# Retention and feed-forward on one core: first products of two blocks by turns, and all weights converted before the second products

## Chip, core and metric

The kernel runs on one core of a Trainium2 chip. The time is the device time of one execution, in microseconds (us); lower is better. The engines named below are PE (TensorE: matmuls), DVE (VectorE), ACT (ScalarE), POOL (GpSimd) and SP (SyncE, which here only issues DMAs).

## What is computed

A retention layer (attention without softmax, with a decay per head) over 8 batches, 8 heads, 576 positions and head size 64, and behind it a feed-forward layer with g = h - tanh(h). All in float32.

```python
def _attn_ref(q, k, v):
    scores = scale * np.matmul(q, k.transpose(0, 1, 3, 2))
    Dmat = np.where(rel >= 0, gamma[:, None, None] ** rel[None, :, :], 0.0)
    return np.matmul(scores * Dmat[None, :, :, :], v)

def _moe_ref(x, w_in, w_out):          # x: 4608 x 512
    h = x @ w_in                       # w_in: 512 x 2048
    g = h - np.tanh(h)
    return g @ w_out                   # w_out: 2048 x 512
```

## The kernel before

**Tiles.** The 576 positions are cut into 9 blocks of 64. One block of all 8 batches is 512 rows of x (`BLK`), kept transposed in two parts, `xh` and `xl`, a rounded value and the rest, since matmuls run on float32r. The 2048 columns of the hidden layer are 16 slices `f` of 128. For block n and slice f there are two groups of twelve 128x512 matmuls: the first product `mm1(n, f)` (line 249: 4 with `xh`, 4 with `xl`, 4 with `xh` and the weight's low part) writes h into a PSUM bank, tag "h", two buffers; the second product `mm2(n, f)` (line 298) adds to four output banks, tags "o0" to "o3". Eight PSUM banks are all there are: two "h", four "o", "new" and "own".

**Attention.** It runs by pairs of batches. `entry(p)` does the 64x64 matmuls of pair p: the outputs and the state of pair p, and the scores of pair p + 1. Then it copies (`after_score`, `after_out`, the state), issues the 1 MB load of pair p + 2 (`load_pair`, line 145; two buffers, so the load waits until pair p's matmuls are done) and has POOL scale q and v of that pair in place (`prep`, lines 154 and 155). Pairs 0 to 3 (block 0) are done by batch ahead of everything (`first_score`, the loop over j). Pairs 4 to 7 give block 1, pairs 8 to 11 block 2.

**Weights.** They arrive as 64-bit numbers and are turned into a high and a low float32r part on the chip, one 128x512 slice at a time: `guard` (two ACT instructions, lines 74 and 75, into a mask), `unit` (DVE, lines 83, 88 and 90, then an ACT cast, line 93), and `finish` (DVE, line 100, the low part), which comes behind the next weight's line 83. A call of `step()` issues a third of that. `stream` is the order: 16 slices of w_in, then 16 of w_out, slices 14 and 15 first (`turn`). `upto("load", n)` issues the loads of raw weights on SP.

**Before the weights are there.** While weights are converted, the first products of blocks 0 and 1 run, and ACT copies each h to SBUF and SP stores it in HBM (`spill`, lines 254 and 255). For (1, 14) and (1, 15) alone `activate` computes g at once. Then come 31 second products: block 1 in the order of `turn`, then block 0 (`late`). `fetch` reads a spilled h back four groups ahead and `resume` computes g, in its parts `gh` and `gl`, one group ahead. From block 2 on first and second products alternate and nothing is spilled.

**What sets the order.** The program is written in the order in which each engine runs it: `in_order` ties each instruction to the one before it on its engine. So an engine that waits holds back all that stands behind it, SP's issues too.

**Names in the change.** `lead`, `seq`: the list of first products by steps k. `bank`: the PSUM tag of h. `scores_of`: the PSUM bank of an entry's scores. `last_two`: the two steps in front of the second products. `ob`, `obs`: the SBUF copy of the output banks; tag "cv", three buffers, is shared with the masks and with `th` of `resume`; tag "xl", two buffers, holds the `xl` of two blocks.

Of the kernel before, what the change touches and what calls it, by code (L numbers as in the profile page):

```python
# [19 lines left out]
P = 128  # L20
# [29 lines left out]
def retention_ffn(ctx: ExitStack, tc: tile.TileContext, ins, out, spill):  # L50
# [57 lines left out]
    def upto(what, n):  # L108
        while at_[what] < min(n, 2 * NF):
            {"load": load_w, "guard": guard}[what](*stream[at_[what]])  # L110
            at_[what] += 1

    def step():

        if not going:
            if at_["convert"] == 2 * NF:
                return finish()
            upto("guard", at_["convert"] + 1)
            going.append(unit(at_["convert"]))
            at_["convert"] += 1  # L120
        if next(going[0], "end") == "end":
            going.pop()

    def units(n):
        while at_["convert"] < min(n, 2 * NF) or going:
            step()
# [32 lines left out]
    def half(k):  # L159
        return slice(64 * k, 64 * k + 64)  # L160
# [79 lines left out]

    gs, ops = {}, {}

    def mm1(n, f):
        hp = psp.tile([P, BLK], F32, tag="h", bufs=2, name=f"h{n}_{f}")
        xh, xl = xs[n]
        k = 0
        for a, x in ((0, xh), (0, xl), (1, xh)):
            for cc in range(NCC):
                nc.tensor.matmul(hp, win[f][:, a, cc, :], x[:, cc, :], start=(k == 0), stop=(k == 3 * NCC - 1))  # L249
                k += 1  # L250
        g = pool.tile([P, BLK], F32, tag="g", bufs=3, name=f"g{n}_{f}")
        if n == 0 or n == 1 and f < NF - 2:

            nc.scalar.copy(g, hp)
            nc.sync.dma_start(spill[n, f], g)
        else:
            activate(n, f, hp, g)
# [27 lines left out]
    def mm2(n, f):  # L285
        gh, gl = gs.pop((n, f))
        first, final = (turn[0], turn[-1]) if n == 1 else (0, NF - 1)
        if f == first:
            ops[n] = [psp.tile([P, DM], F32, tag=f"o{t}", bufs=1, name=f"o{n}_{t}") for t in range(4)]
        o = ops[n]  # L290
        terms = [(gh, 0), (gh, 1), (gl, 0)]
        if f != final:
            order = [(t, k) for k in range(3) for t in range(4)]
        else:
            order = [(t, k) for t in range(4) for k in range(3)]
        for t, k in order:
            g, a = terms[k]
            nc.tensor.matmul(  # L298
                o[t], g[:, t * P : (t + 1) * P], wout[f][:, a, :],
                start=(f == first and k == 0), stop=(f == final and k == 2),  # L300
            )
            if f == final and k == 2:
                ob = pool.tile([P, DM], F32, tag="cv", bufs=3, name=f"ob{n}_{t}")
                if t % 2 == 0:
                    nc.scalar.copy(ob, o[t])
                else:
                    nc.vector.tensor_copy(ob, o[t])
                for u in range(2):
                    nc.sync.dma_start(out[2 * t + u, n * C : (n + 1) * C], ob[half(u)])


    warm = const.tile([P, BLK], BF16, tag="wi15", name="warm")
# [42 lines left out]
    for j in range(B):  # L355
        if j < B - 1:
            first_score(j + 1)
        new = psp.tile([P, 8, D], F32, tag="h", bufs=2, name=f"new_first{j}")[:, :4]
        o = psp.tile([P, 8, C], F32, tag=f"o{2 + j % 2}", bufs=1, name=f"own_first{j}")[:, :4]
        run(m_state(j, new), m_out(j, o))  # L360
        if j < B - 2:
            busy(1, 64)
        if j == B - 1:
            busy(4)
        if 3 <= j < 6:
            step()
        after_out(j, o.unsqueeze(1), 1)
        nc.scalar.copy(state[:, j], new)
    units(2)
    prep(B // 2)  # L370
    prep(B // 2 + 1)

    def scores_of(n, f):

        return psp.tile([P, 2, 4, C], F32, tag=f"o{f % 4}", bufs=1, name=f"s{n}_{f}")

    p = B // 2
    late = [(1, f) for f in turn] + [(0, f) for f in range(NF)]
    for n in range(2):
        for f in range(NF):  # L380
            upto("load", 10 + 3 * f // 4 if n == 0 else NF + 5 + f)
            if n == 0 or f % 4 < 3:
                step()
            if n == 1 and f >= NF - 2:
                fetch(*late[f - NF + 4])
            mm1(n, f)
            if n == 0 or f % 4 < 3:
                step()
                step()
            if n == 0 and f == 2:  # L390
                sc = scores_of(n, f)
                run(m_score(B, sc[:, 0]) + m_score(B + 1, sc[:, 1]), [])
                after_score(B, sc, 2)
            if f in ((5, 8, 11, 14), (1, 5, 9, 13))[n]:
                entry(p, scores_of(n, f))
                p += 1
    for k, (n, f) in enumerate(late):
        for _ in range(2):
            step()
        if 0 < k < len(late) - 1:  # L400
            resume(*late[k + 1])
        if k + 4 < len(late):
            fetch(*late[k + 4])
        if k < len(late) - 1:
            mm2(n, f)

# [63 lines left out]
```

## Time and profile before

| what | value |
|---|---|
| time, median of 3 runs | 911.64 us (911.03 to 911.86) |
| the profiled execution | 914.6 us |
| its span, first to last instruction | 912.8 us |
| PE busy | 882.5 us (97%) |
| DVE / ACT / POOL busy | 369.9 (41%) / 281.1 (31%) / 90.4 (10%) us |
| DMA | 82.06 MB, mean 90 GB/s |
| mean granted clock of PE | 0.992 of full speed |

PE busy, granted clock and DMA rate by stretch:

| stretch, us | PE busy, us | DVE busy, us | granted clock | GB/s |
|---|---|---|---|---|
| 20 to 30 | 6.37 of 10 | 5.24 | 0.83 | 405 |
| 30 to 40 | 7.76 of 10 | 9.65 | 1.00 | 202 |
| 50 to 60 | 9.79 of 10 | 9.58 | 1.00 | 310 |
| 60 to 70 | 9.09 of 10 | 9.24 | 1.00 | 260 |
| 70 to 80 | 8.77 of 10 | 9.20 | 1.00 | 260 |
| 90 to 100 | 10.00 of 10 | 9.15 | 1.00 | 218 |
| 100 to 110 | 7.87 of 10 | 9.84 | 0.86 | 290 |
| 110 to 120 | 10.00 of 10 | 7.82 | 0.97 | 319 |
| 140 to 150 | 7.10 of 10 | 7.32 | 1.00 | 154 |
| 150 to 160 | 7.31 of 10 | 7.76 | 0.83 | 55 |
| 240 to 800 | 560 of 560 | | 1.00 | |

A busy share says little of the whole, since the stages differ: the attention of block 0 ends at about 24 us, first products of blocks 0 and 1 run from 25.46 to 144.22, the 31 second products to 239.76 (from 201.55 on without a gap), and from there first and second products alternate. The chain of waits, followed back from the last instruction, is 86% PE, 7% DVE, 2% ACT and 2% DMA.

### The profile page before, as it was taken

To read this page: it belongs to the slowest core of one execution; us is meant where nothing else is said; L and a number is where in the kernel's file an instruction comes from. 1 tells how busy PE (TensorE), PEld (TensorE's weight loads), DVE (VectorE), ACT (ScalarE), POOL (GpSimd) and SP (SyncE) were. 2 spreads that over 40 slices of the span, in tenths; PEclk is the share of its full clock that TensorE was granted. 3 is DMA by queue.
4 is the path that set the end of the run, shared out by engine and by line. 5 is a ranking of instruction groups with operands and counts; after the bars stand their busy time and mean duration, and the time that the engine had idled before them with its cause. 6 is when DMAs were issued, how large, how long until landed. Compare 5 with 4: busy or idle time off the path is not lost.

```text
span 912.8 us, 17584 instructions
## 1 busy us (share of the span) xinstructions
PE 882.5 (97%) x7832; PEld 722.0 (79%) x7832; DVE 369.9 (41%) x543; ACT 281.1 (31%) x482; POOL 90.4 (10%) x84
## 2 busy tenths in 40 slices
PE   6899997999999999999999999999999999999997
PEld 4677785778888888888888888888888888888885
DVE  3899877545322333223322333223332322223222
ACT  3665554444322222222222222222222222222222
POOL 4212221000011111111111111000111111000000
PEclk9999999999999999999999999999999999999999
DMA  9777783243211113111311131113000211002001
GB/s 355 272 264 246 251 314 105 98 122 105 63 54 52 48 47 93 53 48 47 93 53 47 47 93 53 47 48 93 32 32 38 80 60 47 1 1 47 1 1 46
DMA packets 30524, 82.06 MB, mean 90 GB/s; under 512 B 3696, under 2 KB 4848, under 8 KB 30448
## 3 DMA queue, kind: packets, MB, share of 16 engines
q1 hardware_dynamic: 30448, 80.94, 26.8%
q8 instruction: 61, 1.00, 0.4%
q14 instruction: 15, 0.12, 0.0%
HBM read 63.62 MB, written 17.30 MB: 89 GB/s over the span
## 4 chain that ended last, share of the span: by engine, by line
PE 86%; DVE 7%; ACT 2%; DMA 2%; issue 1%; SPq 1%; POOL 0%; ACTq 0%; DVEq 0%
PE o L298 42%; PE h L249 38%; PE s L191 3%; PE new L191 2%; PE own L191 2%; DMA a<-in_qkv_dram 1%; DVE wi L100 1%; DVE mi L88 1%; DVE mo L90 1%; DMA out_dram<-ob 1%; DVE mo L88 1%; DVE mi L90 1%; DVE wo L100 0%; DVE mi L83 0%; ACT wi L93 0%
## 5 line engine op out<-in xcount | busy, mean ns | idle before, releaser
L249 PE MATMUL h<-xh,wi 128*128 128x512 f32 x1152 | 308.5, 392 | 7.7 <-ACT wi L93 3.8
L298 PE MATMUL o<-wo,gh 128*128 128x512 f32 x1152 | 293.8, 393 | 8.7 <-ACT gh L281 3.7
L249 PEld LDWEIGHTS h<-xh,wi 128*128 128x128 f32 x1152 | 215.3, 188 | 56.3 <-ACT wi L93 5.7
L298 PEld LDWEIGHTS o<-wo,gh 128*128 128x128 f32 x1152 | 214.1, 188 | 56.7 <-ACT gh L281 5.2
L263 DVE TENSOR_TENSOR g<-h,g 128x512 f32<-128x512 f32 x114 | 78.8, 691 | 369.8 <-ACT g L262 369.8
L262 ACT ACTIVATE g<-h 128x512 f32<-128x512 f32 x114 | 68.2, 598 | 424.0 <-PE h L249 424.0
L298 PE MATMUL o<-wo,gl 128*128 128x512 f32 x576 | 159.2, 391 | 0.0
L249 PE MATMUL h<-xl,wi 128*128 128x512 f32 x576 | 154.6, 390 | 0.0
L298 PEld LDWEIGHTS o<-wo,gl 128*128 128x128 f32 x576 | 108.7, 189 | 22.7
L249 PEld LDWEIGHTS h<-xl,wi 128*128 128x128 f32 x576 | 108.3, 188 | 22.8
L265 DVE TENSOR_TENSOR gl<-g,gh 128x512 fp32r<-128x512 f32 x114 | 80.0, 702 | 78.2 <-ACT gh L264 71.4
L154 POOL TENSOR_TENSOR a<-a,qtab 128x512 f32<-128x512 f32 x32 | 42.9, 1339 | 663.2 <-DMA a<-in_qkv_dram 618.4
L264 ACT CAST gh<-g 128x512 fp32r<-128x512 f32 x114 | 70.7, 620 | 87.2 <-DVE g L263 87.2
L191 PE MATMUL own<-a,state 64*64 64x64 f32 x1024 | 63.1, 221 | 0.0
L191 PE MATMUL own<-pm,a 64*64 64x64 f32 x1024 | 61.4, 218 | 0.0
L191 PEld LDWEIGHTS own<-a,state 64*64 64x64 f32 x1024 | 51.2, 135 | 0.4 <-issue 0.4
L191 PEld LDWEIGHTS own<-pm,a 64*64 64x64 f32 x1024 | 51.3, 135 | 0.0
L191 PEld LDWEIGHTS s<-a 64*64 64x64 f32 x1024 | 32.6, 135 | 11.9 <-issue 10.5
L155 POOL TENSOR_TENSOR a<-a,vtab 128x512 f32<-128x512 f32 x32 | 37.8, 1182 | 0.0
L191 PE MATMUL s<-a 64*64 64x64 f32 x1024 | 37.0, 222 | 0.2 <-POOL a L154 0.2
L282 DVE TENSOR_TENSOR gl<-s,gh 128x512 fp32r<-128x512 f32 x30 | 20.8, 692 | 35.5 <-PE o L298 28.1
L191 PE MATMUL new<-a 64*64 64x64 f32 x896 | 30.8, 218 | 0.0
(46 smaller groups left out, 447.4 us busy)
## 6 DMA issues: line engine op xcount, KB each, us to landing
a<-in_qkv_dram SPq DMA_DIRECT2D x32, 1024.0 KB, 5.0
out_dram<-ob SPq DMA_DIRECT2D x72, 128.0 KB, 2.4
rwi<-in_w_in_dram SPq DMA_DIRECT2D x16, 512.0 KB, 9.2
rwo<-in_w_out_dram SPq DMA_DIRECT2D x16, 512.0 KB, 5.5
spill_dram<-g SPq DMA_DIRECT2D x30, 256.0 KB, 3.2
s<-spill_dram SPq DMA_DIRECT2D x30, 256.0 KB, 2.5
a<-in_qkv_dram SPq DMA_DIRECT2D x8, 512.0 KB, 7.6
qtab<-in_qtab_dram SPq DMA_DIRECT2D x9, 128.0 KB, 2.1
```

The lines of the kernel that those rows point to most:

```text
L88: nc.vector.scalar_tensor_tensor(z, lw, 29, z, op0=ALU.logical_shift_right, op1=ALU.bitwise_or)
L90: nc.vector.scalar_tensor_tensor(z, hw, -0x40000000, z, op0=ALU.bitwise_and, op1=ALU.bitwise_or)
L154: nc.gpsimd.tensor_tensor(a[:, :, 0], a[:, :, 0], qtabs[c].unsqueeze(1).broadcast_to([P, 2, 4, C]), op=ALU.mult)
L155: nc.gpsimd.tensor_tensor(a[:, :, 2], a[:, :, 2], vtab[:, c].unsqueeze(1).unsqueeze(3).broadcast_to([P, 2, 4, D]), op=ALU.mult)
L191: nc.tensor.matmul(out_, w, x, start=start, stop=stop)
L249: nc.tensor.matmul(hp, win[f][:, a, cc, :], x[:, cc, :], start=(k == 0), stop=(k == 3 * NCC - 1))
L262: nc.scalar.activation(g, h, AF.Tanh)
L263: nc.vector.tensor_tensor(g, h, g, op=ALU.subtract)
L264: nc.scalar.copy(gh, g)
L265: nc.vector.tensor_tensor(gl, g, gh.bitcast(F32), op=ALU.subtract)
L282: nc.vector.tensor_tensor(gl, g, gh.bitcast(F32), op=ALU.subtract)
L298: nc.tensor.matmul(o[t], g[:, t * P : (t + 1) * P], wout[f][:, a, :], start=(f == first and k == 0), stop=(f == final and k == 2),)
```

## The change

- First products are listed in `seq`: block 0 alone for ten steps, then blocks 0 and 1 by turns, then the last ten of block 1. Each of the 30 steps before the last two issues three calls of `step()`, so all 32 weights are converted (but for the last low part) when the second products begin.
- h goes to four banks in turn up to the fifth last step: the two of "h", and "o2" and "o3", which no second product uses yet. Scores of entries then use only "o0" and "o1".
- Pairs 4 to 7 have their entries behind steps 2, 4, 6 and 9; pairs 8 to 11, before in block 1's first products, behind `late` groups 3, 8, 13 and 18. The scores of the first pair move from step 2 to step 0.
- One raw weight is loaded per step.
- The copies of block 1's and of the last block's outputs get one buffer of four, of tag "xl". The last block's second halves are stored from ACT's queue.
- One conversion step of weight 0 is moved from behind j = 3 to behind the state copy of j = 6.

```diff
-    def mm1(n, f):
-        hp = psp.tile([P, BLK], F32, tag="h", bufs=2, name=f"h{n}_{f}")
+    def mm1(n, f, bank="h"):
+        hp = psp.tile([P, BLK], F32, tag=bank, bufs=2 if bank == "h" else 1, name=f"h{n}_{f}")
...
-                ob = pool.tile([P, DM], F32, tag="cv", bufs=3, name=f"ob{n}_{t}")
+                if n in (1, NC - 1):
+
+                    if t == 0:
+                        obs = pool.tile([P, 4, DM], F32, tag="xl", name=f"ob{n}")
+                    ob = obs[:, t]
+                else:
+                    ob = pool.tile([P, DM], F32, tag="cv", bufs=3, name=f"ob{n}_{t}")
...
-                    nc.sync.dma_start(out[2 * t + u, n * C : (n + 1) * C], ob[half(u)])
+                    queue = nc.scalar if n == NC - 1 and u == 1 else nc.sync
+                    queue.dma_start(out[2 * t + u, n * C : (n + 1) * C], ob[half(u)])
...
-        if 3 <= j < 6:
+        if 4 <= j < 6:
             step()
         after_out(j, o.unsqueeze(1), 1)
         nc.scalar.copy(state[:, j], new)
+        if j == 6:
+            step()
...
+    lead = 10
+    seq = [(0, f) for f in range(lead)]
+    for f in range(lead, NF):
+        seq += [(0, f), (1, f - lead)]
+    seq += [(1, f) for f in range(NF - lead, NF)]
...
+    for k, (n, f) in enumerate(seq):
+        last_two = k - (len(seq) - 2)
+        upto("load", k + 9)
+        if last_two < 0:
+            step()
+        else:
+            fetch(*late[2 + last_two])
+        mm1(n, f, ("h", "o2", "h", "o3")[k % 4] if k < len(seq) - 4 else "h")
+        if last_two < 0:
+            step()
+            step()
+        if k == 0:
+            sc = scores_of(p - 1)
...
+        if k in (2, 4, 6, 9):
+            entry(p, scores_of(p))
+            p += 1
     for k, (n, f) in enumerate(late):
-        for _ in range(2):
-            step()
         if 0 < k < len(late) - 1:
             resume(*late[k + 1])
         if k + 4 < len(late):
             fetch(*late[k + 4])
+        if k >= 4:
+            step()
+        if k in (3, 8, 13, 18):
+            entry(p, psp.tile([P, 2, 4, C], F32, tag="h", bufs=2, name=f"s{n}_{f}"))
+            p += 1
```

The order on PE between the first two entries, before (h0_6 is h of block 0, slice 6; a6 is pair 6's load, own4 pair 4's outputs):

```order
L191 MATMUL own4_616<-pm8_533,a4_117 64x64 x2
L249 MATMUL h0_6_696<-xh0_174,wi6_587 128x512 x4
L249 MATMUL h0_6_696<-xl0_175,wi6_587 128x512 x4
L249 MATMUL h0_6_696<-xh0_174,wi6_587 128x512 x4
L249 MATMUL h0_7_723<-xh0_174,wi7_612 128x512 x4
L249 MATMUL h0_7_723<-xl0_175,wi7_612 128x512 x4
L249 MATMUL h0_7_723<-xh0_174,wi7_612 128x512 x4
L249 MATMUL h0_8_750<-xh0_174,wi8_717 128x512 x4
L249 MATMUL h0_8_750<-xl0_175,wi8_717 128x512 x4
L249 MATMUL h0_8_750<-xh0_174,wi8_717 128x512 x4
L191 MATMUL s0_8_773<-a6_688 64x64 x2
```

And on PE at the same place now (s5 are the scores that entry 5 makes, of pair 6):

```order
L191 MATMUL own4_537<-pm8_479,a4_117 64x64 x2
L249 MATMUL h0_3_617<-xh0_174,wi3_506 128x512 x4
L249 MATMUL h0_3_617<-xl0_175,wi3_506 128x512 x4
L249 MATMUL h0_3_617<-xh0_174,wi3_506 128x512 x4
L249 MATMUL h0_4_644<-xh0_174,wi4_533 128x512 x4
L249 MATMUL h0_4_644<-xl0_175,wi4_533 128x512 x4
L249 MATMUL h0_4_644<-xh0_174,wi4_533 128x512 x4
L191 MATMUL s5_667<-a6_609 64x64 x2
```

Two groups of first products stand between the entries where three did, and they are slices 3 and 4.

On PE from step 10 of the list, now; before, slice 10 of block 0 was followed by slice 11 of block 0:

```order
L249 MATMUL h0_10_1036<-xh0_174,wi10_927 128x512 x4
L249 MATMUL h0_10_1036<-xl0_175,wi10_927 128x512 x4
L249 MATMUL h0_10_1036<-xh0_174,wi10_927 128x512 x4
L249 MATMUL h1_0_1063<-xh1_604,wi0_394 128x512 x4
L249 MATMUL h1_0_1063<-xl1_605,wi0_394 128x512 x4
L249 MATMUL h1_0_1063<-xh1_604,wi0_394 128x512 x4
L249 MATMUL h0_11_1090<-xh0_174,wi11_954 128x512 x4
L249 MATMUL h0_11_1090<-xl0_175,wi11_954 128x512 x4
L249 MATMUL h0_11_1090<-xh0_174,wi11_954 128x512 x4
```

Between two new weights (wi10, wi11) stands now a group with one long converted (wi0).

On DVE at the turn to the second products, before (g1_14 and g1_15 are the last two h of block 1; mo and wo are w_out in conversion; s1_0 the first fetched h):

```order
L263 TENSOR_TENSOR g1_14_1858<-h1_14_1845,g1_14_1858 128x512
L265 TENSOR_TENSOR gl1_14_1860<-g1_14_1858,gh1_14_1859 128x512
L88 SCALAR_TENSOR_TENSOR mo11_1758<-rwo11_1565,mo11_1758 128x512
L90 SCALAR_TENSOR_TENSOR mo11_1758<-rwo11_1565,mo11_1758 128x512
L263 TENSOR_TENSOR g1_15_1887<-h1_15_1874,g1_15_1887 128x512
L265 TENSOR_TENSOR gl1_15_1889<-g1_15_1887,gh1_15_1888 128x512
L83 SCALAR_TENSOR_TENSOR mo12_1865<-rwo12_1670,mo12_1865 128x512
L100 TENSOR_TENSOR wo11_1870<-mo11_1758,wo11_1870 128x512
L88 SCALAR_TENSOR_TENSOR mo12_1865<-rwo12_1670,mo12_1865 128x512
L90 SCALAR_TENSOR_TENSOR mo12_1865<-rwo12_1670,mo12_1865 128x512
L83 SCALAR_TENSOR_TENSOR mo13_1896<-rwo13_1697,mo13_1896 128x512
L100 TENSOR_TENSOR wo12_1919<-mo12_1865,wo12_1919 128x512
```

And on DVE there now:

```order
L88 SCALAR_TENSOR_TENSOR mo13_1528<-rwo13_1383,mo13_1528 128x512
L90 SCALAR_TENSOR_TENSOR mo13_1528<-rwo13_1383,mo13_1528 128x512
L263 TENSOR_TENSOR g1_14_1572<-h1_14_1559,g1_14_1572 128x512
L265 TENSOR_TENSOR gl1_14_1574<-g1_14_1572,gh1_14_1573 128x512
L263 TENSOR_TENSOR g1_15_1594<-h1_15_1581,g1_15_1594 128x512
L265 TENSOR_TENSOR gl1_15_1596<-g1_15_1594,gh1_15_1595 128x512
L280 TENSOR_TENSOR s1_0_1557<-s1_0_1557,th1_0_1621 128x512
L282 TENSOR_TENSOR gl1_0_1620<-s1_0_1557,gh1_0_1619 128x512
```

The conversions of w_out 11 to 13, which stood between and behind the two last activations, stand ahead of them.

## Rows read from the trace of the kernel before

**Rows 1.** Chain of waits, whole span, in order of time: start us, us, what
```profile
250.11 2.95 PE o L298 x12
...
253.06 2.72 PE h L249 x12
...
274.12 2.95 PE o L298 x12
```

**Rows 2.** Timeline of PE, 20 to 40 us: start us, us, instructions, [idle before <-releaser]
```profile
25.46 1.28 PE L249 MATMUL h<-xh,wi 128*128 128x512 f32 x4
...
30.84 1.20 PE L249 MATMUL h<-xh,wi 128*128 128x512 f32 x4 [0.79 <-ACT wi L93]
...
38.26 1.15 PE L191 MATMUL s<-a 64*64 64x64 f32 x32
```

**Rows 3.** Timeline of PE around the entries of block 0
```profile
49.77 1.19 PE L249 MATMUL h<-xh,wi 128*128 128x512 f32 x4
...
58.51 0.27 PE L191 MATMUL s<-a 64*64 64x64 f32 x2 [0.21 <-POOL a L154]
...
84.72 1.19 PE L249 MATMUL h<-xh,wi 128*128 128x512 f32 x4
```

**Rows 4.** Timeline of SP's DMA queue, 30 to 112 us (issues)
```profile
49.94 0.38 SPq L145 DMA_DIRECT2D a<-in_qkv_dram  x1
```

**Rows 5.** Timeline of POOL, 30 to 150 us
```profile
56.97 1.48 POOL L154 TENSOR_TENSOR a<-a,qtab 128x512 f32<-128x512 f32 x1 [23.63 <-DMA a<-in_qkv_dram]
```

**Rows 6.** DMA view, landing of 1 MB loads (L145): at 50, 97, before 20 us
```profile
DMA to landing us min/median/max: 6.9/6.9/6.9
...
DMA to landing us min/median/max: 5.2/5.2/5.2
...
a<-in_qkv_dram SPq DMA_DIRECT2D x2, 1024.0 KB, 11.9
```

**Rows 7.** Timeline of DVE, conversions, 80 to 124 us
```profile
106.00 0.68 DVE L100 TENSOR_TENSOR wo<-mo,wo 128x512 fp32r<-128x512 f32 x1
...
108.69 0.69 DVE L100 TENSOR_TENSOR wo<-mo,wo 128x512 fp32r<-128x512 f32 x1
...
118.49 1.78 DVE L88 SCALAR_TENSOR_TENSOR mo<-rwo,mo 128x512 int32<-128x512 int32 x1
```

**Rows 8.** Timeline of PE, 80 to 130 us
```profile
95.24 1.19 PE L249 MATMUL h<-xh,wi 128*128 128x512 f32 x4
...
105.82 1.20 PE L249 MATMUL h<-xh,wi 128*128 128x512 f32 x4 [2.13 <-ACT g L254]
...
108.25 1.91 PE L249 MATMUL h<-xh,wi 128*128 128x512 f32 x4
...
112.33 1.21 PE L249 MATMUL h<-xh,wi 128*128 128x512 f32 x4
```

**Rows 9.** Timeline of PE, second products of blocks 1 and 0
```profile
144.22 1.98 PE L298 MATMUL o<-wo,gh 128*128 128x512 f32 x8
...
150.13 2.58 PE L298 MATMUL o<-wo,gh 128*128 128x512 f32 x8 [3.03 <-ACT gh L264]
...
156.07 2.11 PE L298 MATMUL o<-wo,gh 128*128 128x512 f32 x8 [1.65 <-ACT gh L281]
...
198.84 1.43 PE L298 MATMUL o<-wo,gh 128*128 128x512 f32 x5 [1.76 <-DVE ob L307]
...
239.76 0.62 PE L249 MATMUL h<-xh,wi 128*128 128x512 f32 x2
```

**Rows 10.** Timeline of ACT, 136 to 165 us
```profile
141.69 0.60 ACT L262 ACTIVATE g<-h 128x512 f32<-128x512 f32 x1 [2.09 <-PE h L249]
...
143.05 0.62 ACT L264 CAST gh<-g 128x512 fp32r<-128x512 f32 x1 [0.76 <-DVE g L263]
```

**Rows 11.** Timeline of SP's DMA queue, 904 us to the end
```profile
905.18 4.94 SPq L309 DMA_DIRECT2D out_dram<-ob  x8
```

**Rows 12.** Busy time by stretch (last columns: PEclk, DMA share, GB/s)
```profile
907.00:907.50 0.50, 0.00 (x0) 0.00 (x0) 0.00 (x0) 0.00 (x0) 0.00 (x0) 1.00 0.98 217
```

More of the change, by code (lines that the diff above doesn't have):

```diff
@@ L371, in retention_ffn, with scores_of @@
     prep(B // 2 + 1)
-    def scores_of(n, f):
-        return psp.tile([P, 2, 4, C], F32, tag=f"o{f % 4}", bufs=1, name=f"s{n}_{f}")
-    p = B // 2
[L378 to L382, printed above, removed]
-                step()
[L384 to L396, printed above, removed]
+    def scores_of(k):
+        return psp.tile([P, 2, 4, C], F32, tag=f"o{k % 2}", bufs=1, name=f"s{k}")
+    lead = 10
[3 more added lines that the diff above has]
+    seq += [(1, f) for f in range(NF - lead, NF)]
+    late = [(1, f) for f in turn] + [(0, f) for f in range(NF)]
+    p = B // 2
+    for k, (n, f) in enumerate(seq):
[11 more added lines that the diff above has]
+            sc = scores_of(p - 1)
+            run(m_score(B, sc[:, 0]) + m_score(B + 1, sc[:, 1]), [])
+            after_score(B, sc, 2)
+        if k in (2, 4, 6, 9):
+            entry(p, scores_of(p))
+            p += 1
     for k, (n, f) in enumerate(late):
-        for _ in range(2):
-            step()
         if 0 < k < len(late) - 1:
```

## Prediction

> **What bounds the kernel now.** I read first the table of busy time by stretch (PE is 97% busy over the span, and without a gap from 240 us to 900 us), then the chain of waits, then the timeline of PE before 240 us, and at each gap the timeline of the engine that released it. From 240 us on nothing but PE's own matmuls stands in the chain [rows 1]: a group of twelve 128x512 matmuls (one `mm1` or one `mm2`) takes 2.72 us, and one that follows an entry (the 64x64 matmuls of a pair's attention) takes 2.95. From one such group to the next, eight groups and one entry, it is 24.01 [rows 1], so an entry costs 24.01 - 8 x 2.72 = 2.25, of which 0.23 falls on the group behind it. The change leaves that stage alone, so what can be won lies before 240 us and after 900.
>
> A ledger of the stretch before 240 us shows what PE loses there, as time less work:
> - first three groups, 25.46 to 38.26 us [rows 2]: 12.80 - 3 x 2.72 = 4.6 lost, waiting for the first three converted weights.
> - nine groups and three entries of block 0, 49.77 to 84.72 [rows 3]: 34.95 - 9 x 2.72 - 3 x 2.25 = 3.7 lost, again on converted weights.
> - four groups and an entry of block 1, 95.24 to 112.33 [rows 8]: 17.09 - 13.13 = 4.0 lost. A wait of 2.13 for a PSUM copy on ACT, and behind it a clock at its lower level: four matmuls take 1.91, where eight take 1.98 in step [rows 8, 9].
> - the 31 second products, 144.22 to 239.76 [rows 9]: 95.54 - 31 x 2.72 = 11.2 lost: a wait of 3.03 for `gh` of (1,15), slow matmuls behind it (2.58 for eight), two waits of 1.65 for the next `gh`, and 1.76 for the copies out of block 1.
> Together 23.5 us.
>
> What feeds PE there is VectorE (DVE). One weight costs it four instructions, 2.69 us from `L100` to the next `L100` [rows 7], against 2.72 for a group, so it has no surplus; and while GpSimd (POOL) prepares a pair, one of the four takes 1.78 instead of 0.68 [rows 7]; over the two POOL instructions of a pair, 2 x 1.48 [rows 5], that is 2.96 x (1 - 0.68/1.78) = 1.8 us lost per pair. Each entry adds three more DVE instructions.
>
> **The change, part by part.**
>
> *Ten steps, then blocks 0 and 1 by turns.* Up to step 9 each group still wants a new weight. From step 10 each new weight serves two groups, so twelve groups want six weights, and DVE, which goes on with one per step, is ahead. The block-0 waits for weights after the last entry cannot recur. The turns themselves issue nothing new.
>
> *Entries earlier, at steps 2, 4, 6 and 9 instead of 5, 8, 11 and 14.* Block 1's x must be there by step 11. This has a price that the old order did not show. An entry scores the next pair, and that pair's 1 MB load is issued only when the entry before it has freed the buffer: the entry ends at 49.77, SP issues at 49.94 [rows 4], the data land 6.9 later, POOL starts at 56.97 and takes 1.48 [rows 5, 6], and the next entry starts at 58.51 after a wait of 0.21 for just that [rows 3]. So the chain is 8.74 long, and three groups (8.16 + 0.23) only just cover it. Two groups give 5.67. With a landing of 6.5 (this one took 6.9, one of the same size at 97 us took 5.2 [rows 6]; the stretch after the change moves about as much per us as the first, so I stay near it) the chain is 8.34: waits of 2.7 at step 4 and 2.7 at step 6. The third period has three groups again, but a new `qtab` is issued ahead of the load, about one issue more (0.4, by [rows 4]): 0.4 wait. Sum 5.8. In these waits DVE converts ahead, so the 3.7 that weights cost there is replaced, not added to. A wait of 2.13 was followed by matmuls at the lower clock level [rows 8], at a cost of about 1.6 in that group; here a slow group before a wait costs nothing, since the load sets the time. I take half of one such loss, 0.8. Sum for this part 6.6 (bounds: 2.8 if the loads land in 5.2 and the clock holds; about 18 more if they land in 11.9, as the two before 20 us do [rows 6]).
>
> *First steps moved.* The last conversion step of weight 0 goes behind the state copy of j = 6, so its cast on ACT comes after DVE has the last but one `xl`; weight 1's masks wait behind it. I count 0.9 later up to step 2. On the other side the first scores move from step 2 into the wait behind step 0 (0.79 [rows 2]) and vanish there, 0.8 saved. The 4.6 becomes 4.7.
>
> *Four banks for h.* The wait of 2.13 came because ACT's copy stood behind a cast that waited for a slowed DVE. With four banks PE runs three groups, over 8 us, ahead of the copies. The 4.0 goes; DVE may run up to that late without PE seeing it. The last four groups use two banks again.
>
> *All of w_out converted by step 29.* The late stage has then only `resume` on DVE and ACT, and PE stands without a gap on these from 201.55 to 239.76. The lag is paid once, at the turn to the second products. I take the lag at the third entry as 1.2, the preparation of the next pair adds 1.8, and twenty steps win back 20 x 0.03 = 0.6: 2.4. `gh` of (1,14) is ready 2.0 after its group (141.69 to 143.67 [rows 10]) and the group behind it covers 2.72, so 0.7 of the lag is free: a wait of 1.7, say 1.8 with the restart. Bounds: 0, and the 3.03 of now with its slow clock, 4.6.
>
> *Four entries moved into the second products.* The same 4 x 2.25 of PE work, only later: nothing gained. Queued behind each is SP's next 1 MB load, which waits for PE, and behind that the next `fetch`; a fetch is wanted three groups later, so 8 us hide it. If not, the wait is of the kind of the 1.65 above.
>
> *Own buffers for the copies of block 1.* The 1.76, and the 0.4 behind it, go; what is left is the copy of the fourth bank ahead of the next group, 0.2, plus 0.2 for restarts.
>
> *The end.* Eight stores are issued by SP one after the other, 905.18 to 910.12 [rows 11]. With half of them on ACT's queue and own buffers the last issue would start near 907.7 instead of 909.5: 1.8 earlier. Against it, the DMA engines are 0.98 busy at 217 GB/s in that stretch [rows 12]; 1.05 MB at that rate takes 4.8, where 5.1 is taken now: 0.3. I take 1.2, nearer to the issues, since a store is issued each 0.62 us and 0.13 MB per 0.62 us is itself about 211 GB/s.
> The Trainium skill, "DMA: Bandwidth & Descriptors", section "Queues, rings and completion order", speaks against this part: SP and ACT each own "one ring on each of the same 16 SDMA engines, not a DMA engine or descriptor generator of their own". By that rule the gain is the 0.3 and the time 0.9 longer than mine.
>
> **Sum.** Losses after: 4.7 + 6.6 + 0 + 1.8 + 0.4 = 13.5, against 23.5: 10.0 gained, with 1.2 at the end 11.2. The profiled execution took 914.6 (span 912.8, and 1.8 around it), so its like would be 903.4; the median of the three runs is 911.64, so I predict 900.4.
>
> **Rivals.**
> - *The loads hide better.* If they land in 5.2, the two waits are 1.4 each and the clock holds: 2.8 instead of 6.6, so 896.6; with no lag at the turn and all 1.8 at the end, 894.2. For it: the loads around 97 us. Against it: 6.9 in the very place.
> - *The lag at the turn is as long as now.* DVE has no surplus, so every delay stays until step 30. A wait of 3.03, the slow clock and two waits of 1.65 give 7.9 instead of 1.8: 906.5.
> - *Conversions do not fit in the first products*, so that the change does not do what it says. 30 weights at 2.69 are 81 us beside 32 groups of 87. If ACT's casts and copies between them stretch a weight to 3.03, 10 us are lost again and the time is about 911. Against it: the 2.69 of [rows 7] has ACT's work in it already.
> - *Slower: the 1 MB loads stand behind the weights.* Weights are now loaded one per step, not 0.75, and entries come every two steps. If the loads land in 11.9 [rows 6], three periods lose 5.4 more each, and two more losses of clock cost 1.6 each: 19 more, 919.8. It decides from a landing of 6.5 + 11.2/3 = 10.2 us. Against it: the load of [rows 4] had weights and spills on the queue too, and about 2.6 MB per period of 10.4 us is 250 GB/s, where the load that took 5.2 ran beside 218 (the stretch 90 to 100 us).
>
> **How the numbers follow.** My forecast 0.48 (897 to 904), loads hidden 0.24, long lag 0.17, conversions not fitting 0.06, loads late 0.05. A range of 894 to 907 leaves out the last two and the tip of the second. This kernel's measurement tells about 0.2%, 1.8 us, from no change. Faster 0.90, same 0.05, slower 0.05.
>
> **What would show it.** Right: PE waits of 2 to 3 us for POOL before the entries at steps 4 and 6, none for `wi` after step 9, none for ACT's copy in the turns; one wait under 2.5 us at the first second products; no wait for `ob`; stores issued on two queues. Wrong: waits for `wi` at steps 10 to 20, a granted clock under 0.9 in several stretches, POOL waiting over 9 us for a load, or PE gaps of over 1 us among the second products after the first three.

## The result and the profile after

The changed kernel takes 901.34 us (median of four runs, 900.30 to 904.46), the kernel before on the same chip 911.51 (911.03 to 911.86): a ratio of 0.9894, 95% interval 0.9870 to 0.9919, so 9.7 us less (7.4 to 11.9). The forecast was 900.4, within 894 to 907.

The page of the kernel after, its span and engine shares:

```profile
span 899.8 us, 17576 instructions
...
PE 878.9 (98%) x7831; PEld 722.4 (80%) x7832; DVE 366.9 (41%) x543; ACT 280.8 (31%) x482; POOL 88.6 (10%) x84
```

PE is still what is busy nearly all the time; only gaps of it can have gone. In the two profiled executions the span shrinks by 13.0 us (912.8 to 899.8). That is more than the timed 9.7, since the profiled execution of before (914.6) stood 3 us above its median and that of after (901.6) at its own. The traces tell where the time went, the timed ratio how much it is.

What PE waited for between 20 and 240 us, kernel after (engine, line, releaser: us in all, times, longest):

```profile
PE s L191 <- POOL a L154: 4.2, 2, 3.0
...
PE h L249 <- ACT wi L93: 1.2, 1, 1.2
PE h L249 <- DVE wi L100: 1.1, 1, 1.1
PE o L298 <- ACT gh L264: 1.0, 1, 1.0
...
PE h L249 <- ACT g L254: 0.3, 1, 0.3
```

The timeline of PE, kernel after, at those places (start us, us, instructions, what ended the idle time before):

```profile
25.44 1.20 PE L249 MATMUL h<-xh,wi 128*128 128x512 f32 x4
...
40.10 1.19 PE L249 MATMUL h<-xh,wi 128*128 128x512 f32 x4
...
47.03 0.27 PE L191 MATMUL s<-a 64*64 64x64 f32 x2 [1.19 <-POOL a L154]
...
57.84 0.27 PE L191 MATMUL s<-a 64*64 64x64 f32 x2 [3.04 <-POOL a L154]
...
60.50 2.07 PE L249 MATMUL h<-xh,wi 128*128 128x512 f32 x4
...
72.07 1.19 PE L249 MATMUL h<-xh,wi 128*128 128x512 f32 x4
...
127.05 1.19 PE L249 MATMUL h<-xh,wi 128*128 128x512 f32 x4 [0.29 <-ACT g L254]
...
133.85 2.11 PE L298 MATMUL o<-wo,gh 128*128 128x512 f32 x8 [1.02 <-ACT gh L264]
...
227.77 1.07 PE L249 MATMUL h<-xh,wi 128*128 128x512 f32 x4
```

Between the first and the last of these rows lie 63 groups and eight entries, 63 x 2.72 + 8 x 2.25 = 189.4 us of work, as before. Time less work is 202.3 - 189.4 = 13.0 lost, where before it was 239.76 - 25.46 - 189.4 = 24.9 [rows 2, 9]. By stretch, with the forecast behind it:

| stretch of after | lost | forecast |
|---|---|---|
| 25.44 to 40.10: three groups, an entry | 14.66 - 10.41 = 4.2 | 4.7 |
| 40.10 to 72.07: seven groups, three entries | 31.97 - 25.79 = 6.2 | 6.6 |
| 72.07 to 133.85: 22 groups | 61.78 - 59.84 = 1.9 | 1.8 |
| 133.85 to 227.77: 31 groups, four entries | 93.92 - 93.32 = 0.6 | 0.4 |

Both counts take the 32 matmuls of the first scores (1.15 us [rows 2]) as lost. The gain sits in the 31 second products, 11.2 lost before [rows 9] and 0.6 now, for 1.9 at the turn to them; between the entries of block 0 more is lost than before, 6.2 against 3.7.

The steady stage begins 12.0 us earlier than before, and the rest from there takes 672.0 instead of 673.0. In the profile, that is: the 24.9 belongs to the one execution of before that was profiled, and a second one lost 21.7 (see the end alone, the last of the experiments). What answers to [rows 4, 5], the issues of the pair loads on SP's queue of the kernel after:

```profile
40.27 0.38 SPq L145 DMA_DIRECT2D a<-in_qkv_dram  x1
...
49.23 0.38 SPq L145 DMA_DIRECT2D a<-in_qkv_dram  x1
```

and POOL's timeline behind them:

```profile
45.55 1.43 POOL L154 TENSOR_TENSOR a<-a,qtab 128x512 f32<-128x512 f32 x1 [12.39 <-DMA a<-in_qkv_dram]
...
56.42 1.37 POOL L154 TENSOR_TENSOR a<-a,qtab 128x512 f32<-128x512 f32 x1 [7.99 <-DMA a<-in_qkv_dram]
```

So from issue to POOL's start it is 5.3 us in one case and 7.2 in the other, then 1.4 on POOL, then the entry. The end of the program, kernel after: the stores on SP's and ACT's queues, and ACT's copy between them, which answer to [rows 11]:

```profile
893.15 3.19 SPq L316 DMA_DIRECT2D out_dram<-ob  x4
893.16 1.42 ACTq L316 DMA_DIRECT2D out_dram<-ob  x2
...
894.62 0.58 ACT L311 COPY ob<-o 128x512 f32<-128x512 f32 x1 [1.49 <-PE o L298]
895.24 1.38 ACTq L316 DMA_DIRECT2D out_dram<-ob  x2
```

and the rate in it, which answers to [rows 12] (stretch, busy time of PE, PEld, DVE, ACT and POOL, granted clock, DMA share, GB/s):

```profile
895.00:895.50 0.50, 0.00 (x0) 0.00 (x0) 0.28 (x1) 0.20 (x1) 0.00 (x0) 1.00 1.08 393
...
897.00:897.50 0.50, 0.00 (x0) 0.00 (x0) 0.00 (x0) 0.00 (x0) 0.00 (x0) 1.00 0.94 348
```

### The profile page after: what moved, and what is told of

The parts are those of the page before. It is cut to its first block, busy times and chain, and to the rows that moved or that the text cites. A ratio compares the mean times of both kernels' runs of the same rounds, so it can differ in the third digit from the quotient of the medians.

```text
span 899.8 us, 17576 instructions
## 1 busy us (share of the span) xinstructions
PE 878.9 (98%) x7831; PEld 722.4 (80%) x7832; DVE 366.9 (41%) x543; ACT 280.8 (31%) x482; POOL 88.6 (10%) x84
## 4 chain that ended last, share of the span: by engine, by line
PE 86%; DVE 7%; ACT 3%; DMA 2%; issue 1%; POOL 0%; SPq 0%; ACTq 0%; POOLq 0%; DVEq 0%
PE o L298 44%; PE h L249 34%; PE s L191 3%; DMA a<-in_qkv_dram 2%; PE new L191 2%; PE own L191 2%; DVE mo L90 1%; DVE wo L100 1%; DVE mo L88 1%; ACT wo L93 1%; DVE wi L100 1%; DVE mi L88 1%; DVE mi L90 1%; DVE mi L83 1%; ACT wi L93 0%
## 5 line engine op out<-in xcount | busy, mean ns | idle before, releaser
L282 DVE TENSOR_TENSOR gl<-s,gh 128x512 fp32r<-128x512 f32 x30 | 23.1, 772 | 29.4 <-PE o L298 16.5
```

The costliest lines, as they stand in the source:

```text
L282: nc.vector.tensor_tensor(gl, g, gh.bitcast(F32), op=ALU.subtract)
```

## The experiments

Where not said otherwise, each is one edit of the kernel after. All are judged by their ratio to the kernel before, run beside them. A difference to the kernel after in us is the difference of the ratios times 911.6; the half-width of one ratio's interval is 0.0009 to 0.0025, so differences between two kernels under some 2.5 us are not told apart by the times, and there only the traces speak. The median of the kernel before differs by 1.4 us from series to series (911.5 to 912.9), its fastest run by 0.6 (910.6 to 911.2), so a difference of ratios carries up to 1.4 us of that; where the plain medians say something else, it stands beside.

**The load chain.** Buffers of their own for pairs 6 and 7, loaded in the first two steps:

```
...
+        if p in (B // 2 + 2, B // 2 + 3):
+            for u in range(2):
+                f = 3 + 2 * (p - B // 2 - 2) + u
+                loaded[2 * p + u] = const.tile([P, 4, 4, C], F32, tag=f"wo{f}", ...)
+                nc.sync.dma_start(loaded[2 * p + u], qkv_d[c, 2 * pr + u])
+            return
...
+        if k in (0, 1):
+            load_pair(B // 2 + 2 + k)
```

> The changed kernel, but pairs 6 and 7 get buffers of their own and are loaded at steps 0 and 1, so that no load stands between an entry and the next; all else the same. Theory (the waits of 1.2 and 3.0 us at steps 4 and 6, and the slow group behind the second, are the 1 MB load that an entry releases): POOL has its data before each entry, both waits and the slow group go, and of the 6.2 us lost between the entries at steps 2 and 9 at least 3 go: 895 to 898 us. Rival (conversions on DVE take the place of the loads, as they bound block 0 in the kernel before, 3.7 us lost there): waits for POOL go, waits for wi appear at steps 6 to 9, and the time stays at 899 to 902.

Measured: 899.54 us, ratio 0.9853 (0.9838 to 0.9868), 3.7 less than the kernel after, or 1.8 by the plain medians; the slowest of its four runs (899.96) is under the fastest of the kernel after (900.30). PE's waits, 20 to 240 us:

```profile
PE h L263 <- DVE wi L100: 2.7, 2, 1.8
PE h L263 <- ACT wi L93: 1.5, 2, 0.8
```

No wait for POOL is left, so the waits before the entries at steps 4 and 6 were the loads. But the stretch that lost 6.2 still loses 3.3 (40.63 to 69.74 us in this trace), 2.4 of it in three waits for converted weights, and some 0.8 more is lost both ahead of it and at the turn: the steady stage begins only 1.4 us earlier. The time is the rival's, and so is the cause; its waits fall at steps 4 and 9.

**The entries spread evenly**, three groups between any two:

```
-        if k in (2, 4, 6, 9):
+        if k in (1, 4, 7, 10):
...
-    lead = 10
+    lead = 11
```

> The changed kernel with the entries of pairs 4 to 7 at steps 1, 4, 7 and 10 instead of 2, 4, 6 and 9, and the turns one step later, so that three groups stand between any two entries. Theory (the waits at steps 4 and 6 are the load chain, 0.2 of issue, 5 to 7 of landing, 1.5 of POOL, which three groups of 8.2 us cover but for 0.5): waits for POOL under 0.6 us each, the 4.2 us and the slow clock of 1.4 behind it gone, and waits for converted weights of 2 to 3 us in their place, since DVE has lost its time to convert ahead: 898.5 to 899.5, as with buffers of their own. Rival (DVE's conversions set the time up to step 9 whatever the entries do, so that the waits for the loads cost nothing): 901.3 as it is, within 1, with waits for wi of 4 us or more.

Measured: 900.70, ratio 0.9867 (0.9848 to 0.9885), 2.5 less than the kernel after by the ratios, which overlap, and 0.6 by the plain medians. PE's waits, 20 to 240 us:

```profile
PE h L249 <- ACT wi L93: 2.1, 3, 0.8
...
PE h L249 <- DVE wi L100: 1.0, 2, 0.5
```

The waits for POOL are gone without any new buffer, as the theory had it, and again conversions take the place. The time, though, lies within the rival's range, and the steady stage begins at 227.56, only 0.2 earlier.

**The first conversion steps back where they were:**

```
-        if 4 <= j < 6:
+        if 3 <= j < 6:
...
-        if j == 6:
-            step()
```

> The changed kernel with the first conversion steps of weight 0 where they were (behind j = 3, 4, 5). The prediction counted 0.9 us of cost for the move: 900.4. Rival (nothing waits for it, the first product starts when xh and xl of the last batch are there): within 0.5 of 901.3.

Measured: 900.63, ratio 0.9882 (0.9867 to 0.9897), 1.1 less; not told apart by the times. The steady stage begins at 226.68, 1.1 earlier. The trace doesn't show that the first steps did it: from the first product to the end of the first entry it loses 4.2 as with the change, though with the granted clock lower at the start (0.50 from 26 to 28 us, 1.00 in the kernel after). Less is lost between the entries, 4.0 against 6.2, in waits for the same loads. What the first steps alone are worth stays open.

**Both edits together** (own buffers, first steps back):

> The changed kernel with two edits together: pairs 6 and 7 in buffers of their own, loaded in the first two steps, and the first conversion steps back where they stood in the kernel before. Theory (the two losses lie in different stretches, 25 to 40 us and 40 to 72 us, and each edit gives what it gave alone, 3.7 and 1.1 us): 4.8 us under the changed kernel's 901.3, about 896.5, a ratio near 0.983, and the steady second products begin near 225 us. Rival (with the load waits gone, PE waits for DVE's conversions from step 0 to step 9 anyway, and what the first steps save is asked back a few groups later): the time of own buffers alone, 899.5, a ratio near 0.9855, with waits for wi of 3 us or more between 30 and 75 us.

Measured: 899.65, ratio 0.9853 (0.9835 to 0.9871), the same as own buffers alone. The rival was right: the gains don't add. DVE's timeline, its last `L100` ahead of the second products:

```profile
127.48 0.69 DVE L100 TENSOR_TENSOR wo<-mo,wo 128x512 fp32r<-128x512 f32 x1
```

and PE's, the first second product:

```profile
132.07 2.11 PE L312 MATMUL o<-wo,gh 128*128 128x512 f32 x8 [1.04 <-ACT gh L278]
```

It is 4.59 from the one to the other. In the kernel after the same two rows are at 129.25 and 133.85, 4.60 apart, with own buffers at 127.77 and 132.37, with the entries spread at 128.98 and 133.58, with the first steps back at 127.98 and 132.58. DVE has little rest ahead of it: it is busy for 98.35 of the 105 us from 25 to 130 with both edits, for 95.11 in the kernel after. Where PE comes later the row does not bind: without the turns (below) PE waits for nothing at its first second product, and it is 5.45 from the one row to the other.

**Two banks for h:**

```
-        mm1(n, f, ("h", "o2", "h", "o3")[k % 4] if k < len(seq) - 4 else "h")
+        mm1(n, f)
```

> The changed kernel with h in the two banks of tag h throughout. Theory (four banks hide copies that ACT makes up to 3 us late, because DVE is late): waits for ACT's copy appear after step 10, PE loses 1 to 4 us there and the wait at the turn to the second products shrinks a little; 902 to 905 us. Rival (the copies keep up without it): within 1 us of the changed kernel's 901.3.

Measured: 901.95, ratio 0.9880 (0.9863 to 0.9898): no cost. PE's only wait of the kind is the 0.3 that four banks have too:

```profile
PE h L249 <- ACT g L254: 0.3, 1, 0.3
```

**No turns** (block 0 whole, then block 1):

```
-    lead = 10
+    lead = NF
...
-    for f in range(lead, NF):
-        seq += [(0, f), (1, f - lead)]
```

> The changed kernel with the first products of block 0 all ahead of those of block 1, no turns; entries, banks and conversions as in the change. Theory of the prediction (turns save what new weights cost in steps 10 to 15): DVE is about 3 us late there and two steps ahead, so PE waits for wi 0.5 to 2 us in all, 902 to 903. Rival (the turns carry the gain of block 0, 3.7 us): 905. Second rival (turns do nothing, since DVE is two weights ahead): 901.3 within 0.7.

Measured: 903.84, ratio 0.9896 (0.9879 to 0.9913), as the kernel after by the ratios, 2.5 more by the plain medians. PE's timeline shows the waits for weights that the turns keep out of block 0; two of four:

```profile
80.69 1.19 PE L249 MATMUL h<-xh,wi 128*128 128x512 f32 x4 [0.78 <-ACT wi L93]
...
85.14 1.19 PE L249 MATMUL h<-xh,wi 128*128 128x512 f32 x4 [0.78 <-ACT wi L93]
```

All four are 0.45 + 0.78 + 0.37 + 0.78 = 2.4 us. In exchange there is no wait at all before the second products.

**Neither turns nor four banks** (the two diffs above together):

> The changed kernel without the turns and with h in two banks; what is left of the change is the entries' places, the conversions ahead, the own buffers and the end. Theory (neither the turns nor the banks carry any of the gain; the 4.0 us of the kernel before at 95 to 112 us went because no entry and no preparation of a pair is left between block 1's first products): 901 to 903, a ratio near 0.990, as without the turns alone. Rival (each stands in for the other: without turns the weights come just in time, so ACT's copies run late and only two more banks keep PE from waiting for them): waits for ACT's copy of g of 2 us and more in block 1's first products, lower clock behind them, 905 to 906, a ratio of 0.9935 or more.

Measured: 901.38, ratio 0.9877 (0.9859 to 0.9896). The theory was right: no wait for a copy on ACT appears, and the time is that of the kernel after within the intervals. In the traces the turns are worth about 1 us: from step 3 to the second products this kernel loses 7.6, and the one with block 1's copies in the shared buffers (below), which up to there is the kernel after and waits 2.2 for the loads as this one does, 6.5.

**Four entries back into block 1's first products:**

```
-        if k in (2, 4, 6, 9):
+        if k in (2, 4, 6, 9, 20, 23, 26, 29):
...
-        if k in (3, 8, 13, 18):
-            entry(p, psp.tile([P, 2, 4, C], F32, tag="h", bufs=2, name=f"s{n}_{f}"))
-            p += 1
```

> The changed kernel with the entries of pairs 8 to 11 behind first products 20, 23, 26 and 29 instead of among the second products. The prediction says of this part that nothing is gained by moving them: 901.3 within 1. Rival (DVE has no surplus in the first products, and each entry adds 2.0 us of DVE work and 1.8 for POOL's preparation): 8 to 15 us more DVE work ahead of the turn, PE waits for ACT copies, for gh and for loads, 907 to 914.

Measured: 907.44, ratio 0.9953 (0.9939 to 0.9967), 5.4 more than the kernel after. PE's timeline:

```profile
113.52 0.32 PE L191 MATMUL s<-a 64*64 64x64 f32 x3 [2.25 <-POOL a L154]
...
118.59 0.26 PE L191 MATMUL new<-a 64*64 64x64 f32 x1 [2.15 <-issue]
...
119.00 2.07 PE L249 MATMUL h<-xh,wi 128*128 128x512 f32 x4
...
141.61 0.33 PE L191 MATMUL s<-a 64*64 64x64 f32 x3 [1.04 <-POOL a L154]
```

The waits are 2.25 + 2.15 + 1.04 = 5.4. Two of the three are the load chain again, and one is idle time that the profile puts down to nothing. Behind the first the granted clock is down, 0.50 from 115 to 124 us, and four matmuls take 2.07 instead of 1.19. So the stretch from step 10 to the second products (70.60 to 149.31) loses 9.9, where it was 1.9: that it is the waits that equal the 5.4 of the times is chance. The time is the rival's; of its waits only those for loads appear. And the entries stand three groups apart here, where the kernel before had four.

**The old pace of conversions** (none in every fourth of the last sixteen steps, the rest ahead of each `resume`):

```
-        if last_two < 0:
+        spare = k >= NF and k % 4 == 3
+        if last_two < 0 and not spare:
             step()
...
     for k, (n, f) in enumerate(late):
+        for _ in range(2):
+            step()
...
```

> The changed kernel with the conversion pace of the kernel before in its last sixteen first products (none in each fourth step), so that two to three weights are left for the second products. Theory (conversions between the last activations made the 7.9 us at the turn): PE waits for gh of (1,15) and of the first fetched slices come back, 5 to 8 us lost there against 1.3 now, 905 to 908. Rival (the wait at the turn is DVE's lag alone, and a pause in each fourth step lets DVE catch up): at most 2 us more, or less, than 901.3.

Measured: 906.09, ratio 0.9926 (0.9906 to 0.9946), 2.9 more, or 4.8 by the plain medians. PE's timeline at the second products:

```profile
134.92 2.11 PE L298 MATMUL o<-wo,gh 128*128 128x512 f32 x8 [0.41 <-ACT gh L264]
...
141.56 3.15 PE L298 MATMUL o<-wo,gh 128*128 128x512 f32 x8 [3.63 <-ACT gh L281]
```

The theory was right. The long wait of before [rows 9] is back, one product later: 0.41 for `gh` of (1,15), where it was 3.03, and 3.63 for that of the first fetched slice (line 281). The clock is down behind it: eight matmuls take 3.15, not 1.98.

**Three weights left for the second products**, on top of both edits, each converted whole behind products 5, 8 and 11:

```
...
-    last, going = [], []
+    last, going, cap = [], [], [2 * NF - 3]
...
-            if at_["convert"] == 2 * NF:
+            if at_["convert"] >= cap[0]:
                 return finish()
...
-        if k >= 4:
-            step()
+        if k in (5, 8, 11):
+            cap[0] += 1
+            for _ in range(3):
+                step()
+            finish()
```

> The two edits as before (pairs 6 and 7 in buffers of their own, first steps back), and the last three weights of w_out, which are wanted only 35 us after the turn, converted among the second products, each whole, behind the fifth, eighth and eleventh product, and not in the first products. It takes 3 x 2.7 = 8.1 us of DVE's work out of the stretch before the turn. Theory (with the loads off the path DVE is the bound there: the second products begin 4.60 us after the last conversion before them in five kernels, and PE waits 1.0 for ACT's copy and 1.0 for gh just ahead of them only because conversions stand before these in DVE's queue): the two waits go, nothing new comes, since DVE has 1.3 us to spare in each second product: 2.0 us under the 899.65 of the two edits, about 897.6, a ratio near 0.983. Rival (ACT, not DVE, makes the two waits, or each late conversion delays gh of the next group as in the kernel with the conversions at the old pace): the same 899.6 or up to 3 us more, with waits for gh of 0.5 us and more among the second products 6 to 13.

Measured: 904.72, ratio 0.9921 (0.9908 to 0.9935), 6.2 more than both edits without it, or 5.1 by the plain medians. PE's timeline:

```profile
130.14 1.98 PE L312 MATMUL o<-wo,gh 128*128 128x512 f32 x8
...
153.28 2.11 PE L312 MATMUL o<-wo,gh 128*128 128x512 f32 x8 [1.68 <-ACT gh L295]
```

Theory and rival are each half right. The second products begin 1.9 earlier than at 132.07, and without a wait, as 2.0 had been expected: DVE is what sets the turn. But the steady stage then begins at 229.45 instead of 226.07, so 5.3 are lost among the second products, 3.9 of them in four waits for `gh`. ACT's timeline at the first shows why:

```profile
150.51 0.62 ACT L93 CAST wo<-mo 128x512 fp32r<-128x512 f32 x1 [3.18 <-DVE mo L90]
...
151.03 0.62 ACT L293 ACTIVATE th<-s 128x512 f32<-128x512 f32 x1
```

The cast stands on ACT for 3.18 us until DVE has the third step of the weight, and the next group's `th` stands behind it. That DVE had time to spare per product did not count; the order of the two queues did. The last 1.4 us of its loss are at the end, where two stores on ACT's queue took 2.88 us to issue instead of 1.42:

```profile
894.74 2.88 ACTq L330 DMA_DIRECT2D out_dram<-ob  x2
...
897.66 0.58 ACT L325 COPY ob<-o 128x512 f32<-128x512 f32 x1 [2.95 <-DVE ob L327]
```

SP's four, issued beside them, took 4.64 instead of 3.19. Why they did is open; the code there is that of the other kernels.

**Block 1's copies in the shared buffers again:**

```
-                if n in (1, NC - 1):
+                if n == NC - 1:
```

> The changed kernel with block 1's output copies in the three shared buffers again. Theory: the waits of 1.76 and 0.4 us behind them come back, 1.8 to 2.2 more, 903.1 to 903.5. Rival (with no conversions beside them, the buffers of tag cv are free sooner): within 0.7 of 901.3.

Measured: 903.57, ratio 0.9914 (0.9897 to 0.9930), 1.8 more, within what the times tell apart. The trace does tell it: in PE's waits stands what had been 1.76 before [rows 9].

```profile
PE o L298 <- DVE ob L313: 2.1, 1, 2.1
```

**The end alone**, as an edit of the kernel before:

```
+                if n == NC - 1:
+                    if t == 0:
+                        obs = pool.tile([P, 4, DM], F32, tag="xl", name=f"ob{n}")
+                    ob = obs[:, t]
...
-                    nc.sync.dma_start(out[2 * t + u, n * C : (n + 1) * C], ob[half(u)])
+                    queue = nc.scalar if n == NC - 1 and u == 1 else nc.sync
+                    queue.dma_start(out[2 * t + u, n * C : (n + 1) * C], ob[half(u)])
```

> The kernel before with only the last block's copies changed: a buffer of their own, second halves stored from ACT's queue. Theory of the prediction (the end is set by issues of 0.62 us on one queue): 1.0 to 1.8 us less than before, 910.1 to 910.5. Rival (the sixteen DMA engines, 0.98 busy at 217 GB/s, set it): 0.3 less, 911.2, and the rate of the last stretch stays near 217 GB/s.

Measured: 910.34, ratio 0.9984 (0.9975 to 0.9993): 1.5 us less (0.6 to 2.3). The queue that issued eight stores in 4.94 us [rows 11] issues four, ACT's the other four, and the rate, for which the rival had 217 GB/s, reaches 369:

```profile
902.00 3.14 SPq L315 DMA_DIRECT2D out_dram<-ob  x4
...
902.00 1.38 ACTq L315 DMA_DIRECT2D out_dram<-ob  x2
...
906.00:906.50 0.50, 0.00 (x0) 0.00 (x0) 0.00 (x0) 0.00 (x0) 0.00 (x0) 0.50 1.03 369
```

The edit changes buffer and queue together, and no run has one without the other. DVE's timeline of the kernel before shows that its last copy had waited for a buffer too:

```profile
908.25 0.69 DVE L307 COPY ob<-o 128x512 f32<-128x512 f32 x1 [2.31 <-DMA out_dram<-ob]
```

Up to 240 us this kernel is the kernel before, executed once more, and so its trace shows which losses of the ledger come again. From its first product at 25.53 us to its steady stage at 236.62 it loses 21.7, not 24.9. The nine groups of block 0 lose 3.7 and the second products 11.3, as before. But the four groups and an entry of block 1 lose 14.44 - 13.13 = 1.3, not 4.0; the wait is half as long and the granted clock stays at 1.00. PE's timeline:

```profile
94.74 1.19 PE L249 MATMUL h<-xh,wi 128*128 128x512 f32 x4
...
104.21 1.20 PE L249 MATMUL h<-xh,wi 128*128 128x512 f32 x4 [1.01 <-ACT g L254]
...
109.18 1.19 PE L249 MATMUL h<-xh,wi 128*128 128x512 f32 x4
```

## Why the prediction was right, and where it was not

The time came out 0.9 us above the forecast, well inside the range, and the four stretches of the table each lie within 0.5 of theirs. Most of the signs named for it are there: waits for POOL before steps 4 and 6 (though 1.19 and 3.04, where 2 to 3 had been said), none for `wi` after step 9, one wait under 2.5 at the turn, stores on two queues. A sign of being wrong is there too, POOL waiting over 9 us for a load: 12.39 at 45.55 us. It was badly chosen, since this idle time counts from POOL's last instruction, and the load was there 5.3 after its issue. Of the single steps:

- *Entries two steps apart cost the load chain: right in kind, and in sum by luck.* 1.19 and 3.04 of waiting instead of 2.7 and 2.7, because the two loads took 5.3 and 7.2 to POOL's start where one value of 6.5 had been taken, and a granted clock of 0.88 from 60 to 70 us, for which 0.8 had been set. 6.2 against 6.6. But one trace is one draw: the four other kernels that have the same instructions up to step 9 (no turns, old pace, entries put back, copies in the shared buffers) lose 6.7, 4.6, 4.6 and 4.9 in this stretch. Buffers of their own and spread entries both take these waits away.
- *"In these waits DVE converts ahead": half right.* It does while PE waits, from 54.80 to 57.84. But the next instruction in its order behind that is the entry's `pm`, and so it stands still for 2.29 us while PE works on the entry. DVE's timeline, kernel after:

```profile
56.70 1.64 DVE L90 SCALAR_TENSOR_TENSOR mi<-rwi,mi 128x512 int32<-128x512 int32 x1
60.62 0.69 DVE L200 TENSOR_TENSOR pm<-s,mask 128x512 f32<-128x512 f32 x1 [2.29 <-PE own L191]
```

  So the longer wait delays the conversions too. Yet the load chain is not worth its full price: with the loads off the path PE waits for DVE instead, and 1.8 to 3.7 of 6.2 come back.
- *First steps moved, 0.9 lost:* the 1.1 of undoing it fits, but the times don't tell it from nothing, its trace has the gain in another stretch, and beside own buffers it gains nothing.
- *"The 4.0 goes" with four banks: it went, but not by the banks, and most of it was not there to win.* With two banks, without turns, and without both, no wait for ACT's copy over 0.3 comes back in that stretch. And a second execution of the same instructions lost 1.3 there, not 4.0: the term was that of the one execution profiled, which took 914.6 where the median is 911.64, and the gain read from it was then taken off the median. With 1.3 in its place the prediction's own sum comes to 8.5 gained and 903.1 us, further off than 900.4. In the traces it is 21.7 less 13.0, and 1.0 to 1.5 at the end: 9.7 to 10.2 gained, as in the times. What was behind the remaining wait, 2.13 in one execution [rows 8] and 1.01 in the other, follows by elimination only: the four entries, and the preparation of pairs that slows DVE, have gone from block 1's first products.
- *"Four entries moved into the second products … nothing gained": not so where three groups stand between entries.* Put back that way they cost 5.4 us. The step looked at the 4 x 2.25 of PE work, which is the same wherever it stands, and did not ask what else the entry brings: its load chain, which three groups cover only just, and its instructions on a DVE without surplus. With the four groups of the kernel before no run puts them back, so what the move gained over it is not measured.
- *Turns:* that the waits for weights cannot recur after step 9 is right; that they are saved by this is so only in part. 2.4 us of them in block 0 without turns, and 0.29 + 1.02 us ahead of the second products with them.
- *The turn to the second products:* 1.8 expected for the wait and its restart, 1.9 lost. The reason is a little simpler than a lag that adds up: wherever PE comes early enough to wait, the second products begin 4.6 us after a fixed conversion row. The rival with a lag as long as now is what the old pace of conversions gives, 2.9 more (4.8 by the plain medians), not 6.1.
- *The ledger of before* had 23.5 lost; over the whole stretch it was 24.9. The parts of it between the four pieces had been taken as free of loss; most of the rest is the first scores' matmuls, which are work.
- *The end:* 1.2 expected, 1.0 in the traces and 1.5 (0.6 to 2.3) measured alone. The rival price of 0.3 had 217 GB/s as the limit of the engines; with two queues they moved 393 and 348 in the rows above. What the Trainium skill, "DMA: Bandwidth & Descriptors", section "Queues, rings and completion order", says of the same 16 engines behind both queues is not touched by this; that they were at their limit at 0.98 busy was the reading that failed.

Undone one at a time, the conversions ahead (2.9), block 1's own buffers (1.8) and the end (1.5) account for 6.2 of the 9.7. The moved entries are the candidate for the rest, less what the load chain costs; that is argued, not measured.

Own buffers for pairs 6 and 7 beat both kernels: 899.54 us, ratio 0.9853, against 0.9894 for the change, with intervals that just fail to meet.

## What to carry to other kernels

When an instruction block is moved, price what it drags along on every queue (its load, the preparation behind it, its place in an in-order vector queue), not its own busy time, which is the same everywhere. Where one engine has no surplus over a long stretch, look for the row at its end that all variants share: savings that don't move that row don't add. Before crediting a saving to an edit, undo that edit alone; here the turns and the four banks carried nothing that the times can show. And before entering a loss in a ledger, look for it in a second execution: here one of four was a third as large in the next.

## What had not been expected of the hardware

- Loads of one size, 1 MB, issued 9 us apart in the same stretch, took 5.3 and 7.2 us from issue to POOL's start.
- A DMA share of 0.98 was no ceiling: the same kind of stores moved 217 GB/s when one queue issued them [rows 12] and up to 393 GB/s when two did, at 1.08, though with stretches of 193 and 213 between (896 to 897 us).
- Issuing a store keeps ACT for about 0.7 us (1.38 to 1.42 for two), and in one kernel 1.44, with ACT's next copy behind it.
- The granted clock fell after a wait of PE of 3.04 us (0.69 from 60 to 64 us, kernel after), after one of 2.25 (0.50 from 115 to 124 us, entries put back) and after one of 3.63 (0.66 from 141 to 146 us, old pace), and not after the 1.19 at 47 us (1.00 from 46 to 50 us, kernel after). The length of the wait alone does not decide it: the clock fell after 2.13 in the kernel before (0.50 from 108 to 110 us), and not after 2.42 with the first steps back (1.00 from 54 to 64 us). The lower level, 0.5, is 1.2 of 2.4 GHz.
